# Attention and soft mixture of experts on one core: another order of the work, one rounding of the maxima, two buffers for low parts, output in 128-row transfers

## The chip, the cores and the metric

The kernel runs on one core of a Trainium2 chip. The time is that of one execution on the device, in microseconds (us), from the first to the last instruction and what lies around them; of several runs the median counts. The core's engines run side by side and wait for each other through semaphores: PE (TensorE, matrix products; PEld is its weight load), DVE (VectorE), ACT (ScalarE), POOL (GpSimd) and SP (SyncE, which here only issues transfers). PE reads the core's memory (SBUF) and writes PSUM, of which six banks of 128 x 512 numbers are handed round here.

## What is computed

Eight batches of eight heads, 576 positions of 64 numbers: attention with a causal mask and a bias that falls with the running sum of `s`; then a soft mixture of eight experts over all 4608 rows, with four slots for each expert.

```python
scores = scale * q @ k.T                       # for each batch and head
cum = cumsum(maximum(s, 0))
scores = where(causal, -1e9, scores + minimum(-(cum_i - cum_j), 0))
attn = softmax(scores);  x = (attn @ v) of all heads side by side   # 4608 x 512
logits = x @ phi                               # 4608 x 32 slots
d = softmax(logits over the rows);   slot_in = d.T @ x              # 32 x 512
h = maximum(slot_in[e] @ w1[e], 0);  slot_out[e] = h @ w2[e]        # 8 experts
out = softmax(logits over the slots) @ slot_out                     # 4608 x 512
```

## The kernel before, in words

Two heads make a pair `p` (32 pairs, four to a batch), one in SBUF rows 0 to 63 and one in rows 64 to 127. The work of a pair is cut into named steps:

- SP `load`: q and k of the pair into `raw` (two buffers). ACT `cast` rounds them into the first half of a `w` buffer; DVE `low` (L354) writes what the rounding lost, the low part, into the second half of the same buffer (three `w` buffers).
- PE `mx` (L383): products whose column maxima DVE takes in `red` (L394). ACT `fh` rounds the maxima, DVE `f0` (L414) takes the lost low part of them, PE `f1` (L430, L435; tiles `mta`, `mtb`) turns them, ACT `f2` copies them out of PSUM and SP `md` writes them as rows into the `g` buffer.
- PE `s` (L472): the scores, four products for each piece: rounded by rounded, low by rounded, rounded by low, and the rows of `g`. ACT `ex` (L483) takes the exponential into a `p` buffer (two of them), POOL `cut` (L490) applies the mask.
- PE `a` (L582, tile `y`, and `ax`, L571, tile `x`): attention times v. POOL `z` (L518 to L524) folds the exponentials for their sums, PE `sm` (L610, tile `sum`) sums them, and both need the `p` buffer until they are done.
- Once for a batch: the sums' reciprocals go through DRAM (`rw`, `rd`), DVE `nr` multiplies, PE `nat`, `lt` turn and multiply with phi, and the slots' steps follow: `t2` (L816, L817: running minimum), `t3` (ACT), `t4` (L835: running sum), `t5` to `t8` (tiles `dn`, `sl`).

The matmuls `mx`, `s` and `f1` use 64 rows of PE at a time, two side by side; all others use 128 rows.

What comes when is set by `schedule()`, which the program runs while it is built: every step has an engine, a length and a priority out of the table `PR`; PE's order is that of the priorities `phase`, `first` and `last`, the other engines take the step that their own rule likes best. Steps of DVE and POOL that use the port that the two share (`port=1`) are put one after the other. Where the plan leaves PE without work before the first `a` and at the end, it sets filler matmuls (`busy`, L1002).

Weights come as 64 quarters of 512 KB: the first `NPRE` into `pre` during attention, others into buffers that attention has done with, the last 15 into quarters that the first expert product has read. Then follow `sit`, the expert products `mlp1` (L1042, tile `m`) and `mlp2` (L1071, tile `m`), `pick` (L1081, tile `sel`), and `result` (L1105, tile `po`): for each half of the columns, ten steps of four matmuls, four copies out of PSUM on DVE and ACT, and one transfer of 512 KB (or two of 64 rows for the last 64 rows of each batch, L1111). The second half of `mlp2` runs between the first steps of `result`:

```python
    m = chain(mlp2(1, 0), mlp2(1, 1))
    steps(m, 1)
    pick(0, m)          # takes two more steps of m, one ahead of each matmul
    steps(m, 2)
    r = result(0)
    steps(r, 2)
    for _ in range(7):
        steps(m, 2)
        steps(r, 1)
```

Of the kernel before, what the change touches and what calls it, by code (L numbers as in the profile page):

```python
# [9 lines left out]
F32 = mybir.dt.float32  # L10
# [7 lines left out]
NEG = -3.0e38  # L18
NG = 3

PR = dict(load=1107.499, load_v=998.6149, cast=(1514.9315, 1120.6562), cum=574.2308,
          low=(1056.8783, 1046.5891), mx=(-317.877, 290.369, -46.176, 247.829),
          red=(417.2219, 179.4465, 326.5474, 121.8857), f0=132.1319, fh=148.805, f1=9.2, f2=352.2992,
          md=535.5937, s=(-354.696, -363.334, -347.782, -83.053), ex=(646.1926, 646.0119, -286.4807, 413.1879),
          cut=(938.5644, 93.0184, 412.4805, 320.3839), zc=416.9435, z=(-64.9653, 613.0481, 538.2899, -206.355),
          ax=228.565, a=(123.859, 345.61, -192.588, 194.944, -117.147), evx=277.8115, ev=989.1526, sm=-132.917,
          e1=314.0294, rw=-208.8097, rd=614.4245, nstep=97.2972, nr=533.0338, nat=258.247, natd=425.8912,
          lt=142.45, nat0=-163.762, natd0=520.9358, c0=419.3522, c1=135.785, soft=1373.0427, mm=608.1714,
          tok=-226.9811, LA=105.3, ct=221.1378, T2=967.0185, LP=1252.0, gap=4.11906,
          endp=(0, 447.3226, 0, 147.8629, 516.6174, -265.6174, -19.1871, 0, 0, 0, 0, 0, -773.6296, 0, 138.2517, 188.4113),  # L30
          endb=(-773.8757, 198.5965, 0, 149.8016, 0, 416.4225, 0, 421.4765, -771.4912, 123.1268, 1041.2334, 0, -226.2111, 0, 370.3865),
          endc=(432.7636, 300.0222, 0, 419.8866, 0, 414.5478, 0, 416.0153, 57.2816, 357.4296, 316.8949, 0, -286.6377, 0, 547.6554),
# [17 lines left out]
def schedule(ops, banks):  # L50
# [21 lines left out]
    while len(start) < len(ops):  # L72
        best = None
        for e, ks in wait.items():
# [4 lines left out]
            for k in ks:  # L79
# [12 lines left out]
                if pick is None or c < pick[0]:  # L92
                    pick = (c, r, k)
            if pick and (best is None or pick[1] < best[0]):
                best = (pick[1], e, pick[2])
# [29 lines left out]
def tile_attn_softmoe(ctx: ExitStack, tc, qk, v, s, phi, w1, w2, cst, out):  # L125
# [79 lines left out]
    for r, h, n in heads:  # L205
        nc.sync.dma_start(out=s_sb[r:r + n], in_=s[h:h + n])
# [1006 lines left out]
```

## Time and profile before

| | us |
|---|---|
| median of 3 runs | 427.53 (425.81 to 427.9) |
| the profiled execution | 424.91 |
| its span, first to last instruction | 423.2 |
| PE busy | 405.0 |
| DVE, POOL, ACT busy | 305.0, 255.0, 254.3 |

The profile has a page with the shares of the engines and the chain of work that ended last, and views that can be asked for: the timeline (instructions in order of time, equal neighbours merged), the windows (busy time in a stretch), the waits, and the instructions of one line. In the profile every 128-row matmul of four-byte numbers shows as two instructions, and a 64-row one as one. A matmul's length is longer than its share of PE, since the next begins while it drains: what a matmul takes of PE is read from start to start.

### The profile page before, as it was taken

To read this page: it belongs to the slowest core of one execution; us is meant where nothing else is said; L and a number is where in the kernel's file an instruction comes from. 1 tells how busy PE (TensorE), PEld (TensorE's weight loads), DVE (VectorE), ACT (ScalarE), POOL (GpSimd) and SP (SyncE) were. 2 spreads that over 40 slices of the span, in tenths; PEclk is the share of its full clock that TensorE was granted. 3 is DMA by queue.
4 is the path that set the end of the run, shared out by engine and by line. 5 is a ranking of instruction groups with operands and counts; after the bars stand their busy time and mean duration, and the time that the engine had idled before them with its cause. 6 is when DMAs were issued, how large, how long until landed. Compare 5 with 4: busy or idle time off the path is not lost.

```text
span 423.2 us, 14675 instructions
## 1 busy us (share of the span) xinstructions
PE 405.0 (96%) x5745; PEld 301.5 (71%) x5745; DVE 305.0 (72%) x1074; ACT 254.3 (60%) x804; POOL 255.0 (60%) x324
## 2 busy tenths in 40 slices
PE   8999999899999999999999999999999999999980
PEld 8877777777788778777878787778777766345450
DVE  7998778769886988688968986897689456121570
ACT  2376776586667657865786577558764655112470
POOL 8468887678768676867687767967657920000000
PEclk9999999999999999999999999999999999999995
DMA  5345436764477247735764574362436989996998
GB/s 180 95 135 168 162 129 187 200 213 132 120 212 246 91 127 227 223 92 140 225 208 115 133 227 139 91 171 59 147 87 172 344 260 409 407 408 246 302 335 255
DMA packets 54217, 82.70 MB, mean 195 GB/s; under 512 B 5404, under 2 KB 41608, under 8 KB 54148
## 3 DMA queue, kind: packets, MB, share of 16 engines
q1 hardware_dynamic: 54148, 81.77, 61.9%
q8 instruction: 45, 0.74, 0.7%
q14 instruction: 24, 0.20, 0.2%
HBM read 71.39 MB, written 10.02 MB: 192 GB/s over the span
## 4 chain that ended last, share of the span: by engine, by line
PE 85%; DVE 4%; DMA 4%; ACT 2%; SPq 1%; issue 1%; DVEq 0%; POOL 0%; POOLq 0%
PE s L472 21%; PE y L582 19%; PE mx L383 13%; PE sum L610 4%; PE m L1071 4%; PE po L1105 3%; PE m L1042 3%; PE nat L651 3%; PE busy L1002 3%; DMA arena<-rs 2%; PE sl L855 2%; PE lt L724 2%; DVE junk L394 1%; DMA arena<-in_qk_dram 1%; PE x L571 1%
## 5 line engine op out<-in xcount | busy, mean ns | idle before, releaser
L483 ACT ACTIVATE arena<-s 128x288 f32<-128x288 f32 (+4 forms) x384 | 120.0, 392 | 43.2 <-PE s L472 41.1
L394 DVE CUSTOM_DVE_ANT_0 junk<-mx,mask 128x448 uint8<-128x448 f32 (+3 forms) x320 | 119.2, 425 | 33.6 <-PE mx L383 33.2
L490 POOL TENSOR_SCALAR_AFFINE_SELECT arena<-arena 128x256 f32<-128x256 f32 (+1 forms) x160 | 69.9, 457 | 68.4 <-ACT arena L483 62.2
L472 PE MATMUL s<-w 64*128 64x288 f32 (+4 forms) x1152 | 105.8, 297 | 0.3 <-DVE mx L394 0.3
L582 PE MATMUL y<-arena 128*64 128x512 f32 (+4 forms) x640 | 97.2, 431 | 0.0
L472 PEld LDWEIGHTS s<-w 64*128 64x128 f32 (+1 forms) x1152 | 84.4, 177 | 4.2 <-DVE mx L394 1.0
L518 POOL TENSOR_TENSOR arena<-arena 128x896 f32<-128x896 f32 x31 | 67.1, 2165 | 11.3 <-PE sum L610 10.5
L582 PEld LDWEIGHTS y<-arena 128*64 128x64 f32 x640 | 39.7, 136 | 36.5 <-issue 27.6
L383 PE MATMUL mx<-w 64*128 64x288 f32 (+4 forms) x384 | 62.2, 320 | 0.3 <-DVE mx L394 0.3
L472 PE MATMUL s<-g 64*128 64x288 f32 (+4 forms) x384 | 58.7, 290 | 0.0
L383 PE MATMUL mx<-g,ones 64*128 64x288 f32 (+4 forms) x384 | 52.8, 299 | 0.0
L354 DVE TENSOR_TENSOR w<-arena,w 128x576 fp32r<-128x576 f32 x64 | 52.2, 833 | 0.4 <-ACT w L349 0.4
L520 POOL TENSOR_TENSOR arena<-arena 128x640 f32<-128x640 f32 x31 | 50.7, 1634 | 2.4
L349 ACT CAST w<-arena 128x576 fp32r<-128x576 f32 x64 | 40.7, 672 | 12.0 <-DMA arena<-in_qk_dram 12.0
L383 PEld LDWEIGHTS mx<-w 64*128 64x128 f32 x384 | 38.4, 184 | 10.4 <-issue 3.8
L383 PEld LDWEIGHTS mx<-g,ones 64*128 64x128 f32 x384 | 38.3, 185 | 0.5
L472 PEld LDWEIGHTS s<-g 64*128 64x128 f32 (+1 forms) x384 | 37.3, 177 | 0.4
L522 POOL TENSOR_TENSOR arena<-arena 128x384 f32<-128x384 f32 x31 | 34.3, 1108 | 1.9
L394 DVE CUSTOM_DVE_ANT_0 junk<-mx,mask,mx 128x288 uint8<-128x288 f32 x64 | 29.9, 505 | 4.7 <-PE mx L383 4.6
L394 DVE DVE_READ_ACCUMULATOR2_ANT mx<- 128x1 f32 x384 | 31.4, 82 | 0.0
L643 DVE TENSOR_TENSOR arena<-arena 128x576 f32<-128x576 f32 x30 | 25.1, 835 | 7.8 <-DMA arena<-rs 7.8
L610 PE MATMUL sum<-arena,onesl 128*32 128x72 f32 x1024 | 22.4, 228 | 0.0
(172 smaller groups left out, 556.8 us busy)
## 6 DMA issues: line engine op xcount, KB each, us to landing
arena<-in_qk_dram SPq DMA_DIRECT2D x32, 576.0 KB
pre<-in_w_dram SPq DMA_DIRECT2D x35, 512.0 KB
arena<-in_w_dram SPq DMA_DIRECT2D x18, 512.0 KB
arena<-rs SPq DMA_DIRECT2D x60, 144.0 KB
arena<-in_v_dram SPq DMA_DIRECT2D x32, 256.0 KB
out_dram<-arena SPq DMA_DIRECT2D x11, 512.0 KB
ww<-in_w_dram SPq DMA_DIRECT2D x7, 512.0 KB
wg<-in_w_dram SPq DMA_DIRECT2D x4, 512.0 KB
```

The costliest lines, as they stand in the source:

```text
L349: nc.scalar.copy(part(i), st["raw", p][:, i, :])
L354: nc.vector.tensor_tensor(part(2 + i), st["raw", p][:, i, :], part(i).bitcast(F32), op=ALU.subtract)
L383: nc.tensor.matmul(ps[a][:, d:d + hi - lo], l[r], t[r, KO + lo:KO + hi], start=t is w, stop=t is gt)
L394: nc.vector.tensor_tensor_reduce(out=junk[:, a, k:k + w], in0=ps[:, d:d + w], in1=mask[:, o:o + w], scale=1.0, scalar=m[:, a, 4:5] if i == ...
L472: nc.tensor.matmul(ps[a][0:n, d:d + hi - lo], t[r, ko + 128 * j:ko + 128 * j + n], t[r, qo + lo:qo + hi], start=x == 0, stop=x == 3)
L483: nc.scalar.activation(st["p", p][0:n, a, o + lo:o + hi], ps[0:n, d:d + hi - lo], AF.Exp, bias=0.0, scale=0.125)
L490: nc.gpsimd.affine_select(d, d, pattern=[[0, 2], [1, n]], compare_op=ALU.is_ge, fill=0.0, base=0, channel_multiplier=-1)
L518: eng.tensor_tensor(z[:, :, 128:576], pt[:, :, 128:576], pt[:, :, 576:1024], op=ALU.add)
L520: eng.tensor_tensor(z[:, :, 256:576], z[:, :, 256:576], pt[:, :, 1024:1344], op=ALU.add)
L522: eng.tensor_tensor(z[:, :, 384:576], z[:, :, 384:576], pt[:, :, 1344:1536], op=ALU.add)
L582: nc.tensor.matmul(y[r, lo - 64:512], vt[:, j, r], st["p", p][:, g, OFF[j] + lo - 128 * j:OFF[j] + 576 - 128 * j], start=(j == 0), stop=(j ...
L610: nc.tensor.matmul(y[o:o + 32, 0:SQ], onesl[:, 31 - 4 * hp - i:63 - 4 * hp - i], st["z", p][:, g, c:c + SQ], start=first and i == 0, stop= ...
```

## The change

- `PR` and all orders in it are new numbers. `schedule()` now picks, among the engines, the step that could start first if the port were free, and the port is given to it.
- The maxima are only rounded: `f0` is gone, `f1` follows `fh`.
- The low parts have buffers of their own (`l`, two of 1152 columns); the three `w` buffers halve. `low` waits for the scores of pair p - 2, where it waited for those of p - 3. The room goes to a 24th early quarter.
- `t2` and `t4` use `tensor_scalar` in place of `scalar_tensor_tensor` and no longer count for the port.
- At the start, memsets go from DVE to POOL and two casts to ACT; three loads of `s` are issued by ACT.
- Rows of odd pairs of batches are cut at other places, so that the output goes in 128-row pieces of 256 KB; the 64-row transfers are gone. `pick` issues its two matmuls at once and takes two steps after them.

```diff
-                r = max(ready[k], f + gap, port if o["port"] else 0)
+                at = max(ready[k], f + gap)
+                r = max(at, port) if o["port"] else at
...
-NBUF = (2, 2, 2, 1, 5, 2, 3)
+NBUF = (2, 2, 2, 1, 5, 2, 3, 2)
-NPRE = 23
+NPRE = 24
...
-        nc.sync.dma_start(out=s_sb[r:r + n], in_=s[h:h + n])
+        nc.scalar.dma_start(out=s_sb[r:r + n], in_=s[h:h + n])
...
-            nc.vector.tensor_tensor(part(2 + i), st["raw", p][:, i, :], part(i).bitcast(F32), op=ALU.subtract)
+            own("l", p, NL)
+            nc.vector.tensor_tensor(lw[:, S * i:S * i + S], st["raw", p][:, i, :], part(i).bitcast(F32), op=ALU.subtract)
...
+        lwar = [("s", p - NL, i) for i in range(4)] if p >= NL else []
-            op(("low", p, i), "DVE", 750, (t0, ("low", i)), (low, i), [("cast", p, i)], port=1)
+            op(("low", p, i), "DVE", 750, (t0, ("low", i)), (low, i), [("cast", p, i)] + lwar, port=1)
...
-        op(("f0", p), "DVE", 160, (tu, "f0"), f0, [("fh", p)], port=1)
-            op(("f1", p), "PE", 110, (tu, "f1"), f1, [("f0", p)], bank=2, mode=1)
+            op(("f1", p), "PE", 110, (tu, "f1"), f1, [("fh", p)], bank=2, mode=1)
...
-            nc.vector.scalar_tensor_tensor(nmin[:, b % 2:b % 2 + 1], mm_[:, 0:1], -1.0, nmin[:, 1 - b % 2:2 - b % 2],
+            nc.vector.tensor_scalar(nmin[:, b % 2:b % 2 + 1], mm_[:, 0:1], -1.0, nmin[:, 1 - b % 2:2 - b % 2],
...
-            next(beside, None)
             nc.tensor.matmul(ps[:, 0:HC], sel[eg], sos[half][:, eg, :], start=(eg == 0), stop=(eg == 1))
         nc.scalar.copy(sl[half], ps[:, 0:HC])
+        steps(beside, 2)
...
+                        nc.sync.dma_start(out=tiles[:, 2 * q + x, c:c + 6:5], in_=ot[:, 2 * x:2 * x + 2])
...
-    steps(m, 1)
     pick(0, m)
-    steps(m, 2)
```

PE, in the middle of attention: where `a` of pair 13 stands before. A row gives the line, the tile written, those read, and the size; `y13` belongs to pair 13, `mx0_16` and `s14` to pairs 16 and 14.

```order
L582 MATMUL y13_2995<-arena_76 64x512 x2
L582 MATMUL y13_2995<-arena_76 64x448 x2
L582 MATMUL y13_2995<-arena_76 64x320 x2
L383 MATMUL mx0_16_0_3013<-w2_143 128x288
...
L472 MATMUL s14_1_0_3042<-g0_131 128x288
L472 MATMUL s14_1_1_3043<-g0_131 128x288
L582 MATMUL y13_2995<-arena_76 64x192 x2
L582 MATMUL y13_2995<-arena_76 64x64 x2
L435 MATMUL mta_3073<-half1_115,mh1_114 128x64
```

What stands in the row now, for the same pair:

```order
L582 MATMUL y13_3204<-arena_72 64x512 x2
L582 MATMUL y13_3204<-arena_72 64x448 x2
L571 MATMUL x13_3220<-arena_72 64x64 x2
L582 MATMUL y13_3204<-arena_72 64x320 x2
L582 MATMUL y13_3204<-arena_72 64x192 x2
L582 MATMUL y13_3204<-arena_72 64x64 x2
L434 MATMUL mta_3231<-half1_108,mh0_106 128x64
```

Before, 36 rows of `mx` and `s` stand between the third and the fourth `y` of the pair, so that PE goes from 128 rows to 64 and back twice; now the `y` of a pair stand together, with only `x` among them. Over all of attention PE turns to 64-row work 80 times before and 56 times now.

DVE, at the maxima of the first pair, before:

```order
L394 ISA mx1_111 128x1
L414 TENSOR_TENSOR mh0_113<-mx0_110,mh0_113 128x2x5
L394 ISA junk_126,mx1_111<-mx0_1_1_261,mask_60 128x288
L394 ISA mx1_111 128x1
L354 TENSOR_TENSOR w2_143<-arena_76,w2_143 128x576
L354 TENSOR_TENSOR w1_141<-arena_76,w1_141 128x576
```

and now:

```order
L356 TENSOR_TENSOR l0_138<-arena_72,w1_134 128x576
L397 ISA junk_119,mx1_104<-mx0_1_0_252,mask_60 128x288
L397 ISA mx1_104 128x1
L397 ISA junk_119,mx0_103<-mx1_0_0_258,mask_60,mx0_103 128x288
L397 ISA mx0_103 128x1
L397 ISA junk_119,mx0_103<-mx1_0_1_259,mask_60,mx0_103 128x288
```

The `f0` of the first pair is gone, and the second `low` of that pair now stands ahead of its last two maxima, where it stood behind them.

PE, from the end of the first half of `mlp2` to the first `po`, before:

```order
L1071 MATMUL m210_7075<-pre_75 32x256 x3
L1081 MATMUL sel0_7080<-pre_75,mask_60 128x256
L1071 MATMUL m210_7075<-arena_76,pre_75 32x256
L1071 MATMUL m210_7075<-pre_75 32x256 x3
L1081 MATMUL sel0_7080<-pre_75,mask_60 128x256
L1071 MATMUL m210_7075<-arena_76,pre_75 32x256
L1071 MATMUL m210_7075<-pre_75 32x256 x7
L1105 MATMUL po0000_7100<-sl0_6996,e_nat_66 128x256
```

and now:

```order
L1073 MATMUL sel0_7051<-pre_71,mask_60 128x256 x2
L1064 MATMUL m210_7055<-arena_72,pre_71 32x256
L1064 MATMUL m210_7055<-pre_71 32x256 x3
L1064 MATMUL m210_7055<-arena_72,pre_71 32x256
L1064 MATMUL m210_7055<-pre_71 32x256 x3
L1098 MATMUL po00000_7064<-sl0_6972,e_nat_66 128x256
```

Four matmuls are one step of `mlp2`. Five steps of its second half stood ahead of the first `po` (the first of them, and a matmul of the second, ahead of the rows shown); now there are two, both behind `sel`.

## Rows read from the trace of the kernel before

**Rows 1.** The page: engines' busy time, and the chain that ended last by engine.

```profile
PE 405.0 (96%) x5745; PEld 301.5 (71%) x5745; DVE 305.0 (72%) x1074; ACT 254.3 (60%) x804; POOL 255.0 (60%) x324
PE 85%; DVE 4%; DMA 4%; ACT 2%; SPq 1%; issue 1%; DVEq 0%; POOL 0%; POOLq 0%
```

**Rows 2.** Windows, one batch: length, busy us (instructions) by engine, clock, DMA, GB/s.

```profile
154.00:195.00 41.00, 41.00 (x624) 32.62 (x616) 33.25 (x124) 28.87 (x95) 30.73 (x37) 1.00 0.61 176
```

**Rows 3.** Timeline of PE: start, length, line, tiles, count; `mx` and `s` use 64 rows.

```profile
141.55 0.29 PE L383 MATMUL mx<-g,ones 64*128 64x288 f32 x2
141.68 0.31 PE L472 MATMUL s<-w 64*64 64x64 f32 x6
...
149.29 0.28 PE L571 MATMUL x<-arena 128*64 128x64 f32 x4
149.51 0.40 PE L383 MATMUL mx<-w 64*128 64x288 f32 x2
149.74 0.29 PE L383 MATMUL mx<-g,ones 64*128 64x288 f32 x2
...
161.12 0.29 PE L472 MATMUL s<-g 64*128 64x288 f32 x2
161.35 0.66 PE L582 MATMUL y<-arena 128*64 128x192 f32 x8
...
171.47 0.28 PE L571 MATMUL x<-arena 128*64 128x64 f32 x4
171.58 1.15 PE L582 MATMUL y<-arena 128*64 128x320 f32 x12
```

**Rows 4.** Timeline at a wait of PE on late copies by ACT.

```profile
320.07 0.24 PE L435 MATMUL mtb<-half,mh 64*128 64x64 f32 x1
...
320.79 0.19 ACT L440 CAST hl<-mta 20x64 fp32r<-20x64 f32 x1
...
320.90 1.06 PE L855 MATMUL sl<-arena,dn 128*32 128x512 f32 x8 [0.58 <-DVE mx L394]
```

**Rows 5.** DVE by line: count, ns min/median/max, first and last start; shapes.

```profile
L817 DVE SCALAR_TENSOR_TENSOR nmin<-mm,nmin x8: 159/1680/1691, 85.9 to 353.0; 128x1 f32<-128x1 f32 x8
L780 DVE TENSOR_SCALAR cs<-cs x8: 171/427/1344, 98.7 to 361.2; 128x5 f32<-128x5 f32 x8
```

**Rows 6.** Timeline of PE behind a long `t2` and `f0`: idle time, and who ended it.

```profile
256.41 0.26 PE L435 MATMUL mta<-half,mh 64*128 64x64 f32 x1 [0.70 <-DVE mh L414]
```

**Rows 7.** The longest wait of ACT in total: us, times, longest.

```profile
ACT arena L483 <- PE s L472: 41.1, 63, 3.5
```

**Rows 8.** Timeline of the start.

```profile
1.44 8.44 PE L1002 MATMUL busy<-ident 128*128 128x128 f32 x48 [1.44 <-POOL ident masks.py:199]
...
8.00 0.81 DVE L262 SCALAR_TENSOR_TENSOR g<-arena,odd 66x576 fp32r<-66x576 f32 x1
...
9.81 0.40 PE L383 MATMUL mx<-w 64*128 64x288 f32 x2
...
15.36 0.17 DVE L414 TENSOR_TENSOR mh<-mx,mh 128x10 fp32r<-128x10 f32 x1
```

**Rows 9.** Chain of waits at the output's start, and SP's first output transfer.

```profile
387.87 1.00 PE m L1071 x16
388.87 0.68 PE po L1105 x8
...
390.35 0.40 SPq L1108 DMA_DIRECT2D out_dram<-ww  x1
```

**Rows 10.** Windows of the output, as in rows 2.

```profile
384.00:386.00 2.00, 2.00 (x41) 0.99 (x33) 0.00 (x0) 0.37 (x1) 0.00 (x0) 1.00 1.05 408
...
398.00:400.00 2.00, 2.00 (x34) 1.05 (x28) 0.77 (x3) 0.95 (x3) 0.00 (x0) 1.00 0.88 248
...
412.00:414.00 2.00, 0.00 (x0) 0.00 (x0) 0.57 (x2) 0.50 (x2) 0.00 (x0) 0.89 0.99 291
414.00:416.00 2.00, 0.00 (x0) 0.00 (x0) 0.00 (x0) 0.00 (x0) 0.00 (x0) 0.50 1.06 364
```

More of the change, by code (lines that the diff above doesn't have):

```diff
@@ L92, in schedule @@
                 if pick is None or c < pick[0]:
-                    pick = (c, r, k)
+                    pick = (c, at if o["port"] else r, k, r)
             if pick and (best is None or pick[1] < best[0]):
-                best = (pick[1], e, pick[2])
+                best = (pick[1], e, pick[2], pick[3])
         if best is None:
             raise ValueError([(k, [a for a in ops[k]['after'] if a not in start]) for k in ops if k not in start][:40])
-        t, e, k = best
+        _, e, k, t = best
         o = ops[k]
@@ L400, in scores @@
             op(("mx", p, i), "PE", mxt[i], (tu, ("mx", i)), (mxp, i),
-               [("cast", p, 0), ("cast", p, 1), dep("f0", old(3))] + cums, bank=2, mode=1)
+               [("cast", p, 0), ("cast", p, 1), dep("fh", old(3))] + cums, bank=2, mode=1)
             for a in range(2):
@@ L834, in t4 @@
         def t4():
-            nc.vector.scalar_tensor_tensor(tot, tot, st["al", b], st.pop(("mm3", b))[:, 1:3], op0=ALU.mult, op1=ALU.add)
+            mm_ = st.pop(("mm3", b))
+            for x in range(2):
+                nc.vector.tensor_scalar(tot[:, x:x + 1], tot[:, x:x + 1], st["al", b], mm_[:, 1 + x:2 + x], op0=ALU.mult, op1=ALU.add)
         def t5():
@@ L865, in batch @@
         op(("t2", b), "DVE", 600, (T, "tok", *late), t2,
-           [("c0", b) if b < B - 1 else ("lt", b * HP + HP - 1), ("t4", b - 1) if b else None], port=1)
+           [("c0", b) if b < B - 1 else ("lt", b * HP + HP - 1), ("t4", b - 1) if b else None])
         op(("t3", b), "ACT", 900, (T + 0.1, "tok", *late), t3, [("t2", b), ("t5", b - 1) if b else None])
-        op(("t4", b), "DVE", 300, (T + 0.2, "tok", *late), t4, [("t3", b)], port=1)
+        op(("t4", b), "DVE", 300, (T + 0.2, "tok", *late), t4, [("t3", b)])
         op(("t5", b), "PE", 218, (T + 0.2, "tok", *late), t5, [("t3", b)], bank=1)
@@ L920, in fetch @@
         nc.sync.dma_start(out=dst, in_=src)
-    for e, ns in (("DVE", 7450), ("POOL", 6500), ("SP", 1500), ("ACT", 2900), ("PE", 1100)):
+    for e, ns in (("DVE", 7300), ("POOL", 7450), ("SP", 1500), ("ACT", 3700), ("PE", 1100)):
         op(("set", e), e, ns, (-1000,), lambda: None)
@@ L927, in tile_attn_softmoe @@
     for i in range(1, NG):
-        op(("gi", i), "POOL", 2400, (2.0 * i - 10,), (ginit, i), [("set", "POOL")])
+        op(("gi", i), "POOL", 2500 if i == 1 else 3700, (2.0 * i - 10,), (ginit, i), [("set", "POOL")])
     for p in range(NP):
@@ L953, in tile_attn_softmoe @@
     room = []
[L954 removed]
+    for kind, n in (("g", NG), ("w", NW), ("l", NL)):
         for i in range(n):
[L957 to L958 removed]
+            room.append(((kind, i, 0), [("s", NP - n + i, y) for y in range(4)]))
     for i in range(o // F):
@@ L990, in tile_attn_softmoe @@
     room.sort(key=lambda r: max([0 if x[0] == "low" else 1 if x[0] == "s" else 3 if x[0] == "t7" else 2 for x in r[1]]))
-    last = None
+    last = {}
     for i, (a, d) in enumerate(room):
-        op(("get", i), "SP", 400, (200.0 + i,), (get, a), d + ([last] if a[0] == "w" else []), dma=1400)
-        if a[0] == "w":
-            last = ("get", i)
+        op(("get", i), "SP", 400, (200.0 + i,), (get, a), d + ([last.get(a[0])] if a[0] != "arena" else []), dma=1400)
+        last[a[0]] = ("get", i)
     def busy(n):
@@ L1002, in busy @@
             nc.tensor.matmul(d[:, 0:128], ident, ident, start=True, stop=True)
-    end = 0
+    end = 2800
     early, after = True, False
```

114 lines of the change are left out of this document (53 added, 61 removed).

## The prediction

> **What bounds the kernel now.** I read the page's shares first: PE is busy 405.0 of 423.2 us and is 85% of the chain that ended last, while DVE, POOL and ACT have a quarter of their time free [rows 1]. A batch in the middle shows the same: in 41 us PE never idles, DVE has 33.3 us of work, POOL 30.7, ACT 28.9, and the DMA engines 0.61 of their time [rows 2]. So until the output begins, a faster DVE is worth something only where PE waits for it, and what counts is what PE is given and in which order. The columns of the matmuls are the same before and after. But PE's time is more than columns. In the timeline I read starts, not lengths. Four `x` matmuls that `y` follows take 0.11 us (171.47 to 171.58); followed by the 64-row `mx` they take 0.22. Inside 64-row work a pair of 288 columns takes 0.13 (141.55 to 141.68); as the first pair after 128-row work it takes 0.23 (149.51 to 149.74), and as the last before it 0.23 (161.12 to 161.35) [rows 3]. A trip into 64-row work and back thus costs 0.11 + 0.10 + 0.10 = 0.31 us, in which PE counts as busy.
>
> At the end another thing binds. From 412 us on PE does nothing and the DMA engines are full, writing the output [rows 10]. That stage ends earlier if it starts earlier, or moves more in a microsecond.
>
> **The order on PE.** 80 trips become 56: 24 x 0.31 = 7.4 us less. The `y` of a pair are no longer split. Changes between `mx` and `s` rise, but at 0.13 us for 288 columns in either they cost nothing [rows 3]. What hid behind this? Bunched 64-row work makes PSUM banks go round faster: every piece of `mx` and `s` takes two of six, given back by DVE and ACT. Where they are late, PE waits. The nearest row is the wait at 320: `mtb` starts at 320.07, ACT copies only at 320.79, PE goes on at 320.90 after 0.58 idle [rows 4]. The new order puts `s` soon after `f1` in every batch. The bounds are none and one such wait for each pair, 32 x 0.58 = 18.6 us. I take three, 1.7 us, as ACT in total waits for PE (41.1 us in 63 waits) and not PE for ACT [rows 7], and since old waits, as that one, can go too.
>
> **Off DVE.** `f0` goes 32 times, the long ones beside POOL. PE waited for one of them, 0.70 us [rows 6]; else the cover is PE's own queue of work. `t2` took up to 1.69 us where its shortest took 0.16, held while POOL worked [rows 5]. DVE idles a fifth of a batch [rows 2], so I cost its relief at 0 (bounds 0 and -2.0, three waits like that one). It is not certain that `t2` and `t4` get any relief: a `tensor_scalar` from SBUF to SBUF is there already, L780, and it takes 0.17 at best and 1.34 at worst [rows 5]. If `t2` is held as before, now where the plan doesn't know it, five batches can each make PE wait 0.70: 3.5 us.
>
> The Trainium skill says (SBUF — State Buffer, Who interferes with whom) that `tensor_scalar` can enter a mode with two ports and then be shut out by GpSimd, as `scalar_tensor_tensor` is with two inputs from SBUF; whether one with a single column in each row does, no row here shows. By that rule the 3.5 us fall due, without it none.
>
> **Two buffers for low parts, 24 early quarters.** `low` now waits for the scores of pair p - 2, and behind it on DVE's queue wait the maxima of later pairs. Between the last `s` of p - 2 and the first of p stand all the matmuls of p - 1, so I cost it at 0; were it short, it would be a wait like that of [rows 6] in each pair. One quarter more in attention lies on DMA engines that are 0.61 busy [rows 2], and takes 512 KB / 408 GB/s = 1.3 us off the full stretch at the end [rows 10].
>
> **The start.** 24 fillers stood ahead of the first `mx`, to 9.88 us; DVE had what `mx` needs at 8.81 [rows 8]. Now 19 stand there (8.44/24 = 0.35 each, 1.8 us less) and DVE has fewer memsets ahead of it. But DVE's maxima follow, and what they gain is less: of the first pair's chain only `f0` (0.17 and its hops) goes for certain. I take 1.0 us; bounds 0 and 1.8.
>
> **The output.** Two steps of `mlp2` in place of five stand ahead of the first `po`; two take 1.00 us, so 1.5 us earlier. The first transfer waited 1.48 us from the first `po` (388.87) to its issue (390.35) for four matmuls and, on each of DVE and ACT, two copies [rows 9]; now one copy each is waited for, which I take as a quarter of it, 0.4. The 64-row transfers are gone: with two of them queued the engines, as busy as ever, moved 291 GB/s where 364 followed [rows 10], so (364 - 291)/364 x 2 us = 0.4 for each of the four places, three of which lie where the DMA binds: 1.2. Sum 3.1, of which I take 3.0, since the second `pick` now has nothing beside its matmuls. Bounds: 1.0, if the transfers of half the size, twice as many, eat the rest; 4.5, if gaps as at 398 (248 GB/s at a share of 0.88) close too [rows 10].
>
> The Trainium skill says (DMA: Bandwidth & Descriptors, Bandwidth) that transfers should be of 1 MiB or more. Its table has 64 KB at 138 GB/s and 1 MB at 341, between which 256 KB would lie under 512 KB. By the row the halves cost nothing, by the rule the stage gets longer; rival 5 has it as a mechanism.
>
> **The sum.** -7.4 + 1.7 - 1.0 - 3.0 = -9.7 us. On the profiled execution, 424.91 us (a span of 423.2 and 1.7 around it), that gives 415.2. That execution lies 2.6 us under the median of the three, so on the median I forecast 427.53 - 9.7 = **417.8 us**.
>
> **The rivals.**
> 1. *The banks take back what the order saves* (0.16). Thirteen waits of 0.58 are 7.5 us; start and output stay: 427.5 - 4.0 = 423.5. For it: [rows 4]. Against: [rows 7], and no idle PE in [rows 2].
> 2. *Slower, by the same banks* (0.10). If ACT's copies are late in most pairs, 28 x 0.58 = 16.2 us stand against 7.4 + 4.0: 432. It decides from 20 pairs on. ACT is busy 28.9 of 41 us [rows 2], which speaks against it; that `s`, `mx` and `f1` now come in long runs, with ACT's share of the work at once, speaks for it.
> 3. *The weights don't come sooner* (0.09). At 384 us they still land at 408 GB/s [rows 10], and the output queues behind them. If their stream doesn't start earlier with the end of attention, only 1.3 us of it, the start's part and the output's 3.0 remain, and some slack ahead of the first `po`: about 421.
> 4. *The slots' steps stay on the port* (0.06): 417.8 + 3.5 = 421.3.
> 5. *Smaller transfers are slower* (0.04): the output, 4608 x 512 numbers or 9.4 MB, takes 32.3 us at 291 GB/s and 25.8 at 364 [rows 10]: 417.8 + 6.5 = 424.3.
>
> The forecast has 0.55. **Range:** downward the full price of everything is 7.4 + 2.0 + 1.8 + 4.5 = 15.7, to 411.8; upward it takes in rivals 1, 3, 4 and 5 and the lower bounds of the start and the output together with rival 1 (427.5 - 0 - 1.0 = 426.5). I give 411 to 426. **Chances:** 0.5% of 427.5 is 2.1 us, about what a measurement of this kernel can tell from no change. Faster, under 425.4: the forecast and most of rivals 1 and 3 to 5, less for what I can't see in an order that is all new, 0.80. Slower, over 429.7: rival 2, 0.10. Between: 0.10.
>
> **What would show it.** A batch in the middle should take some 0.9 us less than its 41 [rows 2], with 64-row work entered six times and not nine, and PE still without idle time. If it is as long and PE's waits name ACT or DVE, rivals 1 and 2 hold. The first output transfer should be issued under 2 us after the first `po`, and some 10 us earlier than 390.35; while PE is idle at the end the rate should stay near 364 GB/s without the dip to 291. `t2` near 0.16 us beside POOL shows the port free, 1.7 shows rival 4. Wrong would be a first `mx` after 9 us, or an output that starts at 386 although PE was ready.

## The result, and the profile after

The changed kernel takes 429.7 us (median of 20 runs) where the kernel before, run beside it, takes 426.4: a ratio of 1.0071, 95% interval 1.0049 to 1.0093. It is slower by 0.7%, some 3 us. The forecast was 9.7 us less.

The profiled execution has a span of 426.1 us; before's had 423.2. The engines' busy times, as in [rows 1], tell nothing of it: PE has the same.

```profile
PE 405.1 (95%) x5739; PEld 301.6 (71%) x5739; DVE 305.4 (72%) x1037; ACT 254.6 (60%) x802; POOL 260.8 (61%) x331
```

The windows say more. The first is one batch, which answers to [rows 2]; the second lies in the output while PE still works, and the others in the stretch in which only the output is left, as the last of [rows 10].

```profile
155.00:197.00 42.00, 41.21 (x615) 31.83 (x614) 34.40 (x117) 29.06 (x94) 31.10 (x36) 1.00 0.59 166
...
408.00:410.00 2.00, 2.00 (x26) 1.27 (x22) 1.51 (x4) 1.33 (x4) 0.00 (x0) 1.00 0.62 206
...
416.00:418.00 2.00, 0.09 (x4) 0.00 (x0) 0.42 (x1) 0.37 (x1) 0.00 (x0) 1.00 1.05 343
418.00:420.00 2.00, 0.00 (x0) 0.00 (x0) 0.00 (x0) 0.00 (x0) 0.00 (x0) 0.98 1.04 337
420.00:422.00 2.00, 0.00 (x0) 0.00 (x0) 0.00 (x0) 0.00 (x0) 0.00 (x0) 0.50 1.05 350
```

PE now idles in attention, 0.79 us in this window, where it had no idle time. With nothing but the output left, the rate is 337 to 350 GB/s without the dip to 291; ahead of that there is a gap that goes lower, 206 GB/s with the DMA engines 0.62 busy. The chain shows where the loss sits: first the line of the kernel before, then those of the changed kernel, with SP's first output transfer from the timeline behind them, as [rows 9].

```profile
359.22 1.09 PE sit L1031 x8
```

```profile
364.35 1.09 PE sit L1024 x8
...
392.51 0.68 PE po L1098 x8
```

```profile
393.65 0.91 SPq L1100 DMA_DIRECT2D out_dram<-ww  x2
```

`sit`, the first product behind attention, starts at 364.35 us; before, it started at 359.22. From there to the end it is 61.8 us, where it was 64.0. So attention lost 5.1 us, and what follows it won 2.2: 1.5 up to the first `po`, 0.4 from there to the first transfer, and 0.4 in the output itself.

**Where in attention.** I took PE's matmuls from 20 us to the first `sit` from start to start (two 64-row matmuls side by side as one step), less their columns at full clock, and sorted what is left. Columns are counted at the full clock, so a stretch at the lower clock shows here too. The absolute value for 128-row work means nothing, so only its difference stands here.

| us | before | after | turns kept | and three `raw` | and half of DVE's and ACT's work |
|---|---|---|---|---|---|
| into and out of 64-row work, and around `f1` | 31.1 | 21.2 | 21.8 | 21.2 | 21.2 |
| at changes between `mx` and `s` | 5.6 | 17.2 | 16.3 | 14.1 | 10.1 |
| elsewhere in 64-row work | 18.1 | 23.7 | 18.3 | 18.7 | 17.2 |
| 128-row work, against before | 0 | -1.9 | -0.5 | -0.2 | -0.8 |

The last three columns are experiments below. The saving on trips is there, and larger than the forecast 7.4: 9.9 us, with 56 entries for 80. It is paid back inside the 64-row work, 11.6 us at changes and 5.6 elsewhere. With 0.3 us won at the start, -9.9 + 11.6 + 5.6 - 1.9 - 0.3 gives the 5.1.

**What PE waits for.** The largest wait, in the timeline at 61 us:

```profile
60.79 2.09 POOL L518 TENSOR_TENSOR arena<-arena 128x896 f32<-128x896 f32 x1
60.99 4.52 DVE L356 TENSOR_TENSOR l<-arena,w 128x576 fp32r<-128x576 f32 x2
...
62.95 1.94 POOL L520 TENSOR_TENSOR arena<-arena 128x640 f32<-128x640 f32 x1
...
64.97 1.39 POOL L522 TENSOR_TENSOR arena<-arena 128x384 f32<-128x384 f32 x1
65.43 0.44 DVE L397 CUSTOM_DVE_ANT_0 junk<-mx,mask 128x288 uint8<-128x288 f32 x1
...
65.94 0.79 PE L386 MATMUL mx<-w 64*128 64x320 f32 x2 [2.02 <-DVE mx L397]
```

POOL begins a fold 0.20 us ahead of DVE's two `low`. They take 4.52 us, where one takes 0.745 at best; the maxima come only at 65.43, and PE stands 2.02 us for a bank that they hold. In the program's plan the order is the other way round. schedule() gives each step a start, and the run can be laid beside it:

```
                      plan            run
low (6, 1)            60.50           60.99 to 63.49
low (6, 0)            61.25           63.42 to 65.51
first fold of pair 4  62.00           60.79 to 62.88
```

POOL came from its last `cut` at 60.8 us and went straight on to the fold, for which the plan lets it wait until 62.00; DVE was 0.49 us late, and nothing in the run holds the fold back until `low` is through. In the plan 49 of the 94 `low` and `nr` end less than 0.4 us ahead of a fold of POOL's; in before's plan it is 27. How far the run lies behind its plan (us, on PE, near a planned time) shows such places as steps:

| kernel | 60 | 70 | 150 | 195 | 235 | 290 | 345 |
|---|---|---|---|---|---|---|---|
| before | 0.6 | 0.3 | 1.2 | 0.5 | 0.0 | 1.0 | 1.4 |
| after | 0.7 | 2.9 | 4.8 | 6.0 | 7.8 | 11.6 | 10.8 |

After's plan starts the last step on the slots' sums at 351.4 us, before's at 356.3. On paper it was 4.9 us better; in the run it is 5.1 worse.

**The clock.** One part of the loss is not waiting. At 285.66 us an `nr` of DVE meets a fold and takes 2.60 us; PE idles 1.48 and then 0.45 us, and right behind that the granted clock is at the lower of its two levels, 1.2 GHz, from 290.2 to 293.6 us. PE is busy all that time, and a pair of 288 columns takes 0.24 us from start to start (290.73 to 290.97), where it took 0.14 just before (286.65 to 286.79):

```profile
285.55 2.10 POOL L518 TENSOR_TENSOR arena<-arena 128x896 f32<-128x896 f32 x1
285.66 2.60 DVE L643 TENSOR_TENSOR arena<-arena 128x576 f32<-128x576 f32 x1 [1.22 <-DMA arena<-rs]
...
286.65 0.30 PE L386 MATMUL mx<-g,ones 64*128 64x288 f32 x2
286.79 0.31 PE L472 MATMUL s<-w 64*128 64x320 f32 x2
...
289.00 0.24 PE L472 MATMUL s<-w 64*64 64x64 f32 x1 [1.48 <-DVE mx L397]
289.69 0.24 PE L472 MATMUL s<-w 64*64 64x64 f32 x1 [0.45 <-DVE mx L397]
...
290.73 0.54 PE L386 MATMUL mx<-w 64*128 64x288 f32 x2
290.97 0.54 PE L386 MATMUL mx<-g,ones 64*128 64x288 f32 x2
```

```profile
290.00:292.00 2.00, 2.00 (x22) 2.00 (x21) 1.91 (x8) 1.00 (x5) 1.59 (x2) 0.55 0.75 166
292.00:294.00 2.00, 2.00 (x22) 1.90 (x21) 0.30 (x3) 0.79 (x3) 0.00 (x0) 0.59 0.95 228
```

That is some 1.7 us (half of 3.4) of the 5.1, all inside 64-row work, in the second and third rows of the table. The kernel before has no such stretch in attention, nor has the run with the turns kept or the one with three `raw` as well.

### The profile page after: what moved, and what is told of

The parts are those of the page before. It is cut to its first block, busy times and chain, and to the rows that moved or that the text cites. A ratio compares the mean times of both kernels' runs of the same rounds, so it can differ in the third digit from the quotient of the medians.

```text
span 426.1 us, 14740 instructions
## 1 busy us (share of the span) xinstructions
PE 405.1 (95%) x5739; PEld 301.6 (71%) x5739; DVE 305.4 (72%) x1037; ACT 254.6 (60%) x802; POOL 260.8 (61%) x331
## 5 line engine op out<-in xcount | busy, mean ns | idle before, releaser
L397 DVE CUSTOM_DVE_ANT_0 junk<-mx,mask 128x320 uint8<-128x320 f32 (+2 forms) x320 | 119.1, 425 | 37.1 <-PE mx L386 33.9
L518 POOL TENSOR_TENSOR arena<-arena 128x896 f32<-128x896 f32 x31 | 66.9, 2159 | 15.0 <-PE sum L610 13.3
L356 DVE TENSOR_TENSOR l<-arena,w 128x576 fp32r<-128x576 f32 x64 | 71.8, 1134 | 2.8 <-PE s L472 2.1
L472 PE MATMUL s<-w 64*128 64x288 f32 (+4 forms) x384 | 68.7, 318 | 2.9 <-DVE mx L397 1.9
L472 PE MATMUL s<-w,l 64*128 64x288 f32 (+4 forms) x384 | 63.4, 294 | 0.0
L472 PE MATMUL s<-l,w 64*128 64x288 f32 (+4 forms) x384 | 62.6, 292 | 0.0
L520 POOL TENSOR_TENSOR arena<-arena 128x640 f32<-128x640 f32 x31 | 57.3, 1848 | 2.4
L386 PEld LDWEIGHTS mx<-w 64*128 64x128 f32 x384 | 43.2, 187 | 11.8 <-DVE mx L397 5.1
L472 PEld LDWEIGHTS s<-w 64*128 64x128 f32 (+1 forms) x384 | 41.6, 178 | 8.3 <-DVE mx L397 3.4
L472 PEld LDWEIGHTS s<-l,w 64*128 64x128 f32 (+1 forms) x384 | 40.6, 178 | 0.3
L472 PEld LDWEIGHTS s<-w,l 64*128 64x128 f32 (+1 forms) x384 | 40.2, 179 | 0.1
```

Source lines behind the costliest of these rows:

```text
L356: nc.vector.tensor_tensor(lw[:, S * i:S * i + S], st["raw", p][:, i, :], part(i).bitcast(F32), op=ALU.subtract)
L386: nc.tensor.matmul(ps[a][:, d:d + hi - lo], l[r], t[r, KO + lo:KO + hi], start=t is w, stop=t is gt)
L397: nc.vector.tensor_tensor_reduce(out=junk[:, a, k:k + w], in0=ps[:, d:d + w], in1=mask[:, o:o + w], scale=1.0, scalar=m[:, a, 4:5] if i == ...
L472: nc.tensor.matmul(ps[a][0:n, d:d + hi - lo], t[r, ko + 128 * j:ko + 128 * j + n], y[r, qo + lo:qo + hi], start=x == 0, stop=x == 3)
L518: eng.tensor_tensor(z[:, :, 128:576], pt[:, :, 128:576], pt[:, :, 576:1024], op=ALU.add)
L520: eng.tensor_tensor(z[:, :, 256:576], z[:, :, 256:576], pt[:, :, 1024:1344], op=ALU.add)
```

## Experiments

Theory A: turns on the port of DVE and POOL are lost in the run. Theory B, the rival that the prediction had: banks. Theories D to G came up on the way; letters are used afresh in some of the expectations, so each says what its letters mean. Times are medians; each ratio is against the kernel before, run beside it.

**1. Turns kept.** POOL may begin a step only when the `low` or `nr` right ahead of it in the plan is through. It does so by a read of one number that this step writes. (The read stands ahead of 28 `cut` as well as of 50 folds, not of folds alone.)

```diff
+    held = None
...
+        if ops[key]["port"]:
+            if ops[key]["eng"] == "POOL" and held and held[0] in ("low", "nr") and t - held[-1] < 1500:
+                nc.gpsimd.tensor_copy(seen, st["u", held[1]][0:1, 0:1] if held[0] == "nr" else
+                                      ls[held[1] % NL][0:1, S * held[2]:S * held[2] + 1].bitcast(F32))
+            held = key + (t + ops[key]["ns"],)
```

> The changed kernel; the only edit is that POOL, ahead of a fold (z) which the plan puts on the port behind a `low` or `nr` of DVE, reads one number that this `low` or `nr` has written, and so waits for it. Theory A (lost turns): the plan puts a fold right behind a `low`, in the run DVE is half a microsecond late, POOL comes first, and `low` lasts 1.3 to 2.7 us where its shortest takes 0.745; the maxima behind it come late and PE waits (61 to 66 us: two `low` take 4.52 us, PE idles 2.02). The changed kernel's run falls 9.6 us behind its own plan between 60 and 300 us, before's run 1.0. With the turns kept most of that should come back, less some waiting of POOL: 421 to 424 us. Theory B (banks): 64-row work in long runs makes PE wait for banks whatever DVE does with the port; then a wait more on POOL gives 429 to 432. Theory C: the price lies elsewhere (two low buffers, slots); then no change, 429 to 431.

Measured: 422.2 us, ratio 0.9917 (0.9883 to 0.9952). A wait more at 78 places on POOL, and some 6.6 us less than the changed kernel (1.0071 - 0.9917 of 426 us). The same place in its timeline:

```profile
60.85 1.42 DVE L356 TENSOR_TENSOR l<-arena,w 128x576 fp32r<-128x576 f32 x2
...
62.34 0.17 POOL L1011 COPY seen<-l 1x1 f32<-1x1 f32 x1 [1.66 <-PE mtb L434]
...
62.48 2.10 POOL L518 TENSOR_TENSOR arena<-arena 128x896 f32<-128x896 f32 x1
```

Two `low` take 1.42 us, and the fold comes after. At 290 us the run lies 6.2 us behind the plan, not 11.6. Theory A holds, B doesn't for this part. Some of the 6.6 us come by the clock: the mean granted clock of the runs is 0.985 in the changed kernel and 0.991 here, and 0.006 of 425 us is 2.6 us, an estimate from these two numbers. By line (count, ns min/median/max), in after and then with the turns kept:

```profile
L356 DVE TENSOR_TENSOR l<-arena,w x64: 745/842/2692, 8.8 to 338.3; 128x576 fp32r<-128x576 f32 x64
L520 POOL TENSOR_TENSOR arena<-arena x31: 1547/1949/2122, 26.8 to 340.2; 128x640 f32<-128x640 f32 x31
```

```profile
L356 DVE TENSOR_TENSOR l<-arena,w x64: 694/785/2526, 8.4 to 333.1; 128x576 fp32r<-128x576 f32 x64
L520 POOL TENSOR_TENSOR arena<-arena x31: 1537/1555/2064, 27.1 to 336.5; 128x640 f32<-128x640 f32 x31
```

Long `low` remain: 2.53 us at most, and 18 of 64 over 1.2 us, where it was 19. The plan has such turns too, with `low` behind a fold. So it isn't the number of held `low` that fell; what a turn costs seems to depend on whether the plan knew of it.

**2. The same on the kernel before**, a control (the edit is the same, with before's place of the low part).

> The kernel before with the same wait as in the run with the turns kept: POOL reads one number of the `low` or `nr` that the plan puts on the port ahead of its fold. Theory A (lost turns): before's run trails its own plan by only 1.0 us between 60 and 300 us, so there is nothing to win back: 424 to 427 us. If the wait does good by itself whatever the order (a fold that starts later leaves DVE more room), it would bring here what it brought the changed kernel, 7 us: 418 us.

Measured: 425.2 us, ratio 0.9997 (0.9966 to 1.0029). Nothing to win where nothing is lost, and the read does no good by itself.

**3 and 4. Before's rule on the new table**, without and with the turns kept.

```diff
-                at = max(ready[k], f + gap)
-                r = max(at, port) if o["port"] else at
+                r = max(ready[k], f + gap, port if o["port"] else 0)
...
-                    pick = (c, at if o["port"] else r, k, r)
+                    pick = (c, r, k)
...
-                best = (pick[1], e, pick[2], pick[3])
+                best = (pick[1], e, pick[2])
```

> The changed kernel with before's rule in schedule(): among the engines the step that starts first, port included, is placed next. PE's order is the same, those of DVE, ACT and POOL are planned anew. The plan then ends attention 5.1 us later (356.6 where it had 351.4), with 18.3 us in which DVE waits for the port, where it had 30.7. If the rule by itself is what costs the run its time (theory A, narrow form), fewer `low` should meet a fold and the run should keep near its plan: some 356.6 + 3 at the first `sit` and 425 us or less. If the collisions come from the table's numbers as well, or if it is the banks, it stays at or above the changed kernel: 429 to 434.

> The changed kernel with before's rule in schedule(), which took 450.8 us and at the first `sit` (384.4 us) was 28 us behind its plan, and with the turns on the port kept by POOL's read. Theory A: most of the 28 us are lost turns, so the run comes near its plan of 356.6 us at the end of attention plus the 6 us that the run with the turns kept had left: 427 to 432 us. If that table and rule are slow for another reason (banks, PE's colder clock, late transfers): 445 us or more.

Measured: 450.8 us without (ratio 1.0577, 1.0526 to 1.0628), 426.8 with (1.0036, 1.0004 to 1.0069). The narrow form of theory A, that the rule is to blame, falls: with before's rule this table runs worse. The wide form gets its strongest support: the same read takes off 24 us, and the run's lag at 290 us goes from 23.7 to 5.6. One of the three alike places of the first (153, 199, 245 us), in its timeline, and the window right behind it:

```profile
150.19 2.09 POOL L517 TENSOR_TENSOR arena<-arena 128x896 f32<-128x896 f32 x1
150.53 4.37 DVE L355 TENSOR_TENSOR l<-arena,w 128x576 fp32r<-128x576 f32 x2
...
155.71 0.42 PE L385 MATMUL mx<-w 64*128 64x288 f32 x1 [2.59 <-DVE acc L864]
```

```profile
156.00:158.00 2.00, 2.00 (x23) 2.00 (x22) 1.78 (x9) 0.28 (x2) 0.31 (x1) 0.50 0.86 280
```

The clock is at 1.2 GHz behind the wait. Before the first `sit` there are five such stretches in this trace, 20.5 us in all, and two in that of the second, 6.8 us; half of the difference, some 7 us, is an estimate of what the lower clock has of the 24. So a lost turn can cost twice: by the wait, and by the clock behind it.

**5. Three low buffers in the run alone** (turns kept; the plan still thinks of two).

```diff
-NBUF = (2, 2, 2, 1, 5, 2, 3, 2)
+NBUF = (2, 2, 2, 1, 5, 2, 3, 3)
-NPRE = 24
+NPRE = 23
-        lwar = [("s", p - NL, i) for i in range(4)] if p >= NL else []
+        lwar = [("s", p - 2, i) for i in range(4)] if p >= 2 else []
```

> The run with the turns kept, with three buffers for the low parts and 23 early quarters in place of two and 24; the plan still lets `low` wait for the scores of pair p - 2, so the order of DVE's and PE's work is the same and only the wait itself goes. The prediction costed this wait at 0. In the changed kernel DVE stood at it four times for 3.6 us in all (1.26 at 282.4), with the turns kept once for 0.57. If it costs 0 there: 421 to 424 us. If the second buffer is what is short: under 420.

Measured: 424.1 us, ratio 0.9968 (0.9936 to 0.9999). Nothing is won, and `sit` comes at 359.5 us, as in number 1 (359.6): the wait itself costs nothing. It could not show what follows from it, since DVE's and SP's orders stayed as they were.

**6 and 7. Is it DVE that holds the banks?** Turns kept and maxima over half the columns (they are wrong), and the control on the kernel before.

```diff
-                w = hi - lo
+                w = (hi - lo) // 2
```

> The run with the turns kept, with maxima over half of the columns of each piece, so the maxima are wrong and DVE has some 70 us less work; the order of everything is unchanged. From 20 us to the first `sit`, PE's steps at a change between `mx` and `s` take 16.3 us more than their columns there, 5.6 in the kernel before. Theory A (banks): PE waits there, mostly under 0.25 us at a time, for banks that DVE's maxima still hold; given back sooner, most of the 11 us go: 411 to 416 us, and the 16.3 fall under 8. Theory B: a change from `mx` to `s` or back costs PE that time by itself; then the 16.3 stay and the time hardly moves: 419 to 422.

> The control: the kernel before with maxima over half of the columns (they are wrong), all orders unchanged. Theory A (banks): here PE hardly waits for them, 5.6 us at all changes between `mx` and `s` and 1.8 in waits of 128-row work, so 2 to 4 us go: 421.5 to 424. If DVE's load binds this kernel as it does the changed one, it falls as far as that: 415 to 419.

Measured: 421.3 us (0.9894, 0.9867 to 0.9922) and 424.5 (0.9979, 0.9953 to 1.0005). DVE is busy 252.3 us, where it was 298.8 with the turns kept, and the steps at changes still take 15.9 us, where the theory of banks wanted under 8. Attention ends 3.5 us earlier (356.1 for 359.6), not 11; part of that is lost again to a lower clock behind `sit` (last section). DVE's hold alone isn't it.

**8 to 10. Late q and k.** With two low buffers `low` waits for the scores of p - 2, so the `raw` buffer comes free later, and the plan issues q and k 4.7 us ahead of their `cast` (median of pairs 4 to 31), where before's had 11.2. With the turns kept, at 198.67 (1.03 us of PE's time):

```profile
198.67 1.24 ACT L350 CAST w<-arena 128x576 fp32r<-128x576 f32 x2 [1.44 <-DMA arena<-in_qk_dram]
...
199.97 0.40 PE L386 MATMUL mx<-w 64*128 64x288 f32 x2 [1.03 <-ACT w L350]
```

A third `raw` buffer with the turns kept and without, and a third low buffer that the plan knows (turns kept):

```diff
-NBUF = (2, 2, 2, 1, 5, 2, 3, 2)
+NBUF = (3, 2, 2, 1, 5, 2, 3, 2)
-NPRE = 24
+NPRE = 23
```

> The run with the turns kept, with three `raw` buffers for q and k in place of two (23 early quarters); the plan knows it, and issues a pair's q and k 14.6 us ahead of their `cast` (median of pairs 4 to 31) where the changed kernel's plan has 4.7 and before's 11.2. Theory D (late q and k): since `low` waits for the scores of p - 2, the `raw` buffer comes free late and q and k land just when they are needed; ACT waits for them 20 times for 20.8 us, and PE behind it at changes between `mx` and `s`. With the third buffer that goes: the 16.3 us at those changes fall to 12 or less, attention ends 3 to 5 us earlier, 417 to 420 us (the plan itself is 0.9 us longer). Theory E: the waits at the changes are the price of this order on PE itself, and q and k only fill time that PE would lose anyway: 421 to 424.

> The changed kernel with three `raw` buffers and 23 early quarters, without the read that keeps the turns. It separates the two causes: if late q and k are what makes DVE late and turns are lost only because of it, this alone should win as much as with the turns kept, 417 to 421 us. If turns are lost anyway, it stays near the changed kernel less the 3 to 5 us: 425 to 428 us.

> The run with the turns kept, with three buffers for the low parts that the plan knows of (23 early quarters), so that DVE's `low` stands earlier in its order and q and k are issued 13.9 us ahead of their `cast`. The plan by itself is 5.1 us longer (356.5 for 351.4), as the table was made for two. Theory D: the run falls behind this plan by 2 to 3 us, not 6, and takes 420 to 424 us. Theory E: it falls behind by 6 as before, and 426 to 429 us come out.

Measured: 421.2 us (0.9905, 0.9867 to 0.9943), 426.1 (1.0008, 0.9979 to 1.0038) and 425.5 (1.0012, 0.9981 to 1.0043). The waits of ACT for q and k, in all (us, times, longest), in after, with the turns kept, and with three `raw` as well:

```profile
ACT w L350 <- DMA arena<-in_qk_dram: 15.6, 14, 2.4
```

```profile
ACT w L350 <- DMA arena<-in_qk_dram: 20.8, 20, 2.8
```

```profile
ACT w L350 <- DMA arena<-in_qk_dram: 3.7, 3, 1.8
```

The waits go, `sit` comes 1.9 us earlier (357.7), the steps at changes fall to 14.1. Theory D is right in kind and half as large as expected; the two times with the turns kept (numbers 1 and 8) can't be told apart. The turns and the loads are two causes: the third buffer by itself wins 0.6% (1.0071 to 1.0008), and the read on top of it another 1.0%. A third buffer also gives a new plan, though, with other orders on DVE, ACT and POOL; no run here parts the two. The third low buffer bears D out in its lag, 2.5 us at 290, but its plan is 5.1 us longer, which eats the gain.

**11 and 12. What banks cost in all.** As number 8, with exponentials over half the columns from pair 2 on, then with the maxima halved too.

```diff
+                hi = hi if p < NPB else lo + (hi - lo) // 2
                 nc.scalar.activation(st["p", p][0:n, a, o + lo:o + hi], ps[0:n, d:d + hi - lo],
```

> The run with three raw buffers and the turns kept, with ACT's exponentials from pair 2 on over half of the columns of each piece (the other half keeps old numbers, so the result is not the attention). ACT gives the banks of `s` back sooner; the order of everything is unchanged. With the turns kept and q and k early, PE's steps at changes between `mx` and `s` still take 14.1 us more than their columns, where before's take 5.6. Theory F (banks of `s`): ACT holds them, as in the wait at 320 us of the kernel before; then the 14.1 fall to 8 or less and some 4 to 6 us go: 415 to 417.5 us. Theory G: what is left there is not a matter of banks; the time stays within 1.5 us: 419.5 to 422.

> As the run beside it, with the maxima too over half of the columns (they are wrong): both engines that hold PE's banks have less work. It bounds what banks cost in this order in all. Theory F, for both engines together: the 14.1 us at changes fall to 6, as in the kernel before, and the time to 412 to 416 us. Theory G: the 14.1 stay above 11, and not more than 3 us go in all, 418 to 421.

Measured: 419.5 us (0.9872, 0.9830 to 0.9915) and 419.3 (0.9857, 0.9813 to 0.9900). The steps at changes take 13.3 and 10.1 us, and `sit` comes at 355.6 and 353.3. So banks are at most 4.0 of the 8.5 us that still lay above before's 5.6, and only when both engines are faster (halved work makes everything else of these engines earlier too). The time doesn't follow in number 12: its `sit` comes 2.3 us earlier than number 11's, but the clock falls at 354.8 us, and it takes 29.7 us to the first `po` and not 28.1. The other 4.5 stay open: of its 256 steps at changes 41 take 0.06 to 0.12 us too long, 4.0 us in all, where the kernel before has 12 of 196 with 1.1; no run here tells why.

**13. `f0` alone.** The kernel before without it.

```diff
-            mh = st["mh", p]
-            nc.vector.tensor_tensor(mh[:, :, 1, :], m, mh[:, :, 0, :].bitcast(F32), op=ALU.subtract)
+            pass
```

> The kernel before with `f0` not written (the plan still leaves 160 ns for each): the order of all other work is unchanged, and the maxima go in rounded, as in the changed kernel. DVE loses 32 instructions and 14.9 us, among them five or so of 1.0 to 1.5 us held beside POOL's folds. The prediction costed this at 0, with 2.0 us at most: 424.4 to 426.4 us. A rival: DVE's slack matters more than PE's waits for it show, and 3 us or more go: under 423.

Measured: 424.1 us, ratio 0.9952 (0.9916 to 0.9987): 2.0 us, the far end of my bound (by the interval 0.6 to 3.6).

**14. The output alone** (the hunks of the diff on `MAIN` and `REST`, `result`, `pick` and the steps around them, on the kernel before).

> The kernel before with the changed kernel's output alone: rows of odd batches cut at the other places, transfers of 256 KB in 128 rows, `pick` ahead of two steps of `mlp2`. Attention is as before, but for the places of the rows. The prediction has 3.0 us for this, bounds 1.0 and 4.5, so 423.4 us (421.9 to 425.4). In the changed kernel's trace the stretch from the first `sit` to the end is 61.8 us where it was 64.0, so 2.2 us less: by that 424.2. If the output is no better by itself and the 2.2 came from weights that had landed relatively earlier (they had 5 us more), nothing changes: 426.

Measured: 423.1 us, ratio 0.9945 (0.9915 to 0.9975): 2.3 us.

**15. The slots' steps as before**, in the changed kernel.

```diff
-            nc.vector.tensor_scalar(nmin[:, b % 2:b % 2 + 1], mm_[:, 0:1], -1.0, nmin[:, 1 - b % 2:2 - b % 2],
-                                    op0=ALU.mult, op1=ALU.min)
+            nc.vector.scalar_tensor_tensor(nmin[:, b % 2:b % 2 + 1], mm_[:, 0:1], -1.0, nmin[:, 1 - b % 2:2 - b % 2],
+                                           op0=ALU.mult, op1=ALU.min)
...
-            for x in range(2):
-                nc.vector.tensor_scalar(tot[:, x:x + 1], tot[:, x:x + 1], st["al", b], mm_[:, 1 + x:2 + x], op0=ALU.mult, op1=ALU.add)
+            nc.vector.scalar_tensor_tensor(tot, tot, st["al", b], mm_[:, 1:3], op0=ALU.mult, op1=ALU.add)
```

> The changed kernel with `t2` and `t4` written as scalar_tensor_tensor, as before, the plan unchanged, so they are not planned for the port. In the changed kernel `t2` takes 0.21 us while POOL folds (213.73), where before it took 1.68. If the slots' steps off the port are worth something: 3.5 us more by the prediction's rival 4, which had 0.70 for each of five batches, so 432 to 434 us, and `t2` back at 1.7. If DVE's slack hides it: 428.5 to 431.

Measured: 431.6 us, ratio 1.0160 (1.0124 to 1.0196), 0.9% over the changed kernel's. `t2`, in after and in this run:

```profile
L817 DVE TENSOR_SCALAR nmin<-mm,nmin x8: 211/213/215, 85.5 to 358.1; 128x1 f32<-128x1 f32 x8
```

```profile
L817 DVE SCALAR_TENSOR_TENSOR nmin<-mm,nmin x8: 159/986/1128, 86.7 to 358.2; 128x1 f32<-128x1 f32 x8
```

The hold comes back, up to 1.13 us. But this run's profiled execution, the fastest of its four, has the changed kernel's span, 426.1 us, with `sit` at 364.4: where the 0.9% sits, the profile doesn't show.

**16. The parts that won, on the kernel before**: numbers 13 and 14 together.

> The kernel before, its order and table untouched, with the two parts of the change that measured faster alone: `f0` not written (0.9952) and the changed kernel's output (0.9945). They lie in different stages. If they add up: 0.9952 x 0.9945 = 0.9897, so 421 us, as fast as the changed kernel with the turns kept (0.9917). If the output's start is bound by the weights, the earlier end of attention is lost there: 0.9945, 423.1 us.

Measured: 422.5 us, ratio 0.9934 (0.9910 to 0.9957). The product of the two, 0.9897, lies just under the interval, so they don't quite add up. The lowest time with all the work done is number 8's, the changed kernel with its turns kept and a third `raw` buffer: 421.2 us, under both kernels. By their intervals numbers 1 and 16 can't be told from it.

## Why the prediction was wrong

The step that failed is the one that moved `low`. I asked only who stands behind `low` on DVE's queue, put the move at 0, gave the port's new rule no price, and left 1.7 us for all waits of PE inside 64-row work. There the runs show 17.2 us. Keeping the turns on the port alone takes 6.6 us off the time, which makes the changed kernel faster than the kernel before. In the profiled executions the terms are -9.9 for the trips, +17.2, -1.9 in 128-row work (for which the sum had no term), -0.3 at the start and -2.2 behind attention, in all +2.9 us, which is the difference of the spans.

Point by point:

- **Trips (-7.4).** Right in kind and a third larger: 9.9 us less. [rows 3] gave the price.
- **Waits for banks (+1.7, bounds 0 and 18.6).** The term that was mis-sized: 11.6 us at changes and 5.6 elsewhere, 17.2, near the upper bound. I had the rival for it, "the banks take back what the order saves", and held [rows 7] and [rows 2] against it. Those are sums of a kernel in which DVE and ACT had their own order; how late they come is set by that order, and it was new. And most of the 17.2 isn't banks as such: some 6 are lost turns (1.7 of them the lower clock), 2 late q and k, up to 5 are banks, and the rest is open (the columns of the table, from left to right). Rival 2's 432 us lies closest to the result, but by another way: it had ACT's copies behind `f1` late, and the runs show DVE and its port in the main.
- **"I cost its relief at 0", as DVE idles a fifth of a batch.** Wrong: `f0` alone is worth 2.0, and the slots' steps put back on the port cost 0.9% (number 15). A fifth of free time in a batch doesn't say that PE never waits; the wait of [rows 6] was one such place.
- **Two buffers for low parts, "so I cost it at 0".** The step that failed. The wait is free, as number 5 shows. But `low` also gives back `raw`, so q and k came just in time; and it was planned close ahead of a fold, where at 61 us half a microsecond of lateness cost PE two.
- **The port given by arrival** had no price in my sum at all. The rows were there: [rows 5] shows a step of DVE lasting as long as POOL's, and I used them for `t2` alone, not for the 64 `low`.
- **`t2` and `t4`.** That the port lets go of `t2` is right: 0.21 beside a fold at 213.73. Rival 4 falls. `tensor_scalar` on one column isn't held in any of the seven cases beside a fold (0.21 us in each); the five columns of L780 are, 1.73 us beside a fold (below), where they take 0.17 at best. The rule of the Trainium skill (SBUF — State Buffer, Who interferes with whom) is that `tensor_scalar` can enter a two-port mode and then contend with GpSimd. The five columns agree with it; the one column doesn't show it. The same section of the Trainium skill says that an instruction of DVE with two inputs from SBUF contends with GpSimd's reads, and of the two-port mode that whoever issues first has the pair for the whole instruction. The rows at 60.79 agree with the first: the first `low` ends 0.61 us behind the fold that began ahead of it. The rows of L780 agree with the second: it ends 0.04 us behind the fold. Those are the sentences that I should have set against this change.

```profile
103.59 2.60 POOL L518 TENSOR_TENSOR arena<-arena 128x896 f32<-128x896 f32 x1
104.50 1.73 DVE L780 TENSOR_SCALAR cs<-cs 128x5 f32<-128x5 f32 x1
```

- **The start (-1.0).** The first `mx` comes at 8.46, before 9 us as asked, but the weights of its second half wait for `g`, and `s` gains 0.3. Near the lower bound.

```profile
8.46 0.41 PE L386 MATMUL mx<-w 64*128 64x320 f32 x2
...
8.96 0.19 PEld L386 LDWEIGHTS mx<-g,ones 64*128 64x128 f32 x2 [0.31 <-DVE g L260]
```

- **The output (-3.0, bounds 1.0 and 4.5).** Right within its bounds: 2.3 alone, 2.2 in the spans. From `sit` to the first `po` it is 28.1 us for 29.6, as the 1.5 said; the first transfer follows 1.1 us behind `po`, for 1.5, as the 0.4 said. What fell short is the 1.2 for the 64-row transfers: from the first transfer to the end it is 32.4 us for 32.8, 0.4 less: the dip to 291 went, but a gap like that at 408 us came. Rival 5 falls: 337 to 350 GB/s with 256 KB. The rule of the Trainium skill (DMA: Bandwidth & Descriptors, Bandwidth) is to batch transfers to 1 MiB or more. It doesn't show between 512 and 256 KB; no run here moves 1 MiB at once.
- **Weights (rival 3).** Not seen: with `sit` at 355.6 (number 11) it is still 28.1 us to the first `po`.

By the marks that I set: the batch should have taken 0.9 us less, PE should not idle; the window of one batch is 42 us and PE idles in it, and the waits name DVE and ACT, which was the mark for rivals 1 and 2.

## What to carry to other kernels

A planned order of two engines on a shared resource is no order in the run: if the plan puts a long step of one right behind a short step of the other, write the wait down, or the first half microsecond of lateness turns them round and costs the long step. If PE stands idle behind it, look at the granted clock too: here it fell behind such waits, and PE paid a second time. When a step is moved later, price every buffer that it gives back, up to the transfer that fills it, not only the queue that it stands in. And a plan's own times are a profile: laid beside the run, the places where the lag jumps are the places to look at.

## What the runs showed of the hardware

- The hold goes both ways: L520, 1.55 us alone, has a median of 1.95 us in the changed kernel, where `low` slips in between the folds (62.95 us above); with the turns kept it is 1.56.
- Inside 64-row work the first pair of `mx` or `s` behind `f1` takes 0.10 us more than its columns in the changed kernel (median 0.096 for 21 pairs of `mx`, 0.097 for 8 of `s`), about what the first `mx` behind 128-row work does (0.12). In its price, `f1` ahead of `mx` is like a second entry.
- The granted clock fell to 1.2 GHz behind PE's idle times in attention, as shown at 290 us in the changed kernel and at 156 us in number 3, but not behind every one: in the changed kernel it stayed at 2.4 GHz behind the 2.02 us at 66 us. In number 6 it fell behind the 0.73 us idle of PE ahead of `sit` (a mean of 0.74 in the window, part of it at 1.2 GHz), in number 11 it did not behind the same; the first took 29.7 us from `sit` to the first `po`, the second 28.1. The two windows, of number 6 and of number 11:

```profile
355.00:360.00 5.00, 4.03 (x26) 1.90 (x28) 1.56 (x7) 0.99 (x3) 0.46 (x1) 0.74 1.03 407
```

```profile
355.00:360.00 5.00, 4.18 (x38) 2.13 (x42) 1.10 (x6) 0.76 (x3) 0.46 (x1) 1.00 1.03 410
```
